# Square sums of q in PSUM, all of w_in converted during the scores, and three folds ahead of the layers, in a fused attention and feed-forward kernel

## The chip, the cores and the metric

One core of a Trainium2 chip runs the whole kernel. The metric is device time in microseconds (us), median of the timed runs. The engines are named as in the profile: PE (TensorE, matmuls), ACT (ScalarE), DVE (VectorE), POOL (GpSimd) and SP (SyncE, which issues every DMA of this kernel).

## The reference

Four batches of channel attention, with q, k and v of 6,080 tokens by 256 channels, then a layer pair of width 2,048 over all 24,320 tokens:

```python
def _attn_ref(q, k, v, tau):
    qn = q / (np.linalg.norm(q, axis=1, keepdims=True) + 1e-06)
    kn = k / (np.linalg.norm(k, axis=1, keepdims=True) + 1e-06)
    s = kn.transpose(0, 2, 1) @ qn / tau
    s = s - s.max(-1, keepdims=True)
    a = np.exp(s)
    a /= a.sum(-1, keepdims=True) + 1e-09
    return (v @ a).astype(np.float32)

def _moe_ref(x, w_in, w_out):
    h = x @ w_in
    g = h - np.tanh(h)
    return (g @ w_out).astype(np.float32)
```

The norms run over the tokens, so they need the squares of all of q and k of a batch summed up: these are the square sums of this text. w_in and w_out come in 64-bit floats.

## The kernel before

**Folding.** The kernel never computes v @ a. For each batch it multiplies the softmax e with w_in (a *fold*, `fold`, L270), one of eight column groups s of w_in at a time, and applies the result to v. A fold's result goes from PSUM (ps_w) to fx (L602), gets four sums on DVE (L608 to L611), and is split into a rounded upper half (L616, ACT) and the rest (L620, DVE). Both lie in f, a ring of three SBUF tiles, and are kept in DRAM (f_d) for the later token blocks.

**Quads.** The layers run in 192 quads: four batches, six pairs of token blocks of up to 512 columns, eight column groups. A quad makes seven products p1 to p7 of three matmuls each from f and the split V (vh, vl), by Strassen's scheme, in three PSUM banks x, y and z. ACT copies partial sums out (p, u), DVE adds (c), ACT takes tanh (t), DVE subtracts, ACT rounds (gh), DVE takes the rest (gl), and 24 matmuls with w_out add to ps_o. The list `ORDER` says in which order a quad's products stand on PE and where the side work (scores of the next batch, folds) goes.

**Converting.** w_in and w_out are turned from 64-bit to a pair of 32-bit floats on the chip (`Convert`), in eight pieces each. A piece is loaded (raw), ACT takes a magnitude (L313), DVE runs an upper part of three operations (L318, L320, L321) and a lower part of two (L327, L328), POOL adds (L331), ACT rounds (L334), POOL takes the rest (L337). A converted piece of w_in is stored to DRAM (wi_d, L354) and loaded again (L357) where its tile is needed in between.

**The first batch.** PE computes the scores of batch 0 in plain float32 (`plain_step`: 25 groups of up to two steps, 4 matmuls a step in the profile), as q and k come in. ACT squares each group in place (L415, L418). The squares are added up group by group: those of q on POOL into an SBUF tile (accq), those of k on DVE into PSUM bank 3 (acck), both at L424. ACT then copies acck to SBUF (L429), and 8 small matmuls per accumulator sum over the partitions (ps_n, L436). From these DVE computes the norms (x, y, z, r), a diagonal matrix (diag), PE spreads it (ps_b, L541), and the softmax and its transposes (ps_t) follow. In between PE runs steps of batch 1's scores, by `fill(n)`. Then come folds 0 and 1 and the first quad.

**Early pieces.** During the scores of batch 0 the pieces 2, 3, 0, 1, 4 and 5 of w_in are asked for, into a ring of three tiles `wi`. Folds 2 to 7 run inside quads 0 to 5.

**What sets the order.** `Plan` lists all operations with an estimated cost (`pe_cost`, `dve_cost` and so on) and a due time, and `order` writes each engine's instructions in the order in which its own small model would start them. The engines execute that order; each waits at an instruction until its inputs are there and its output tile is free. SP too takes its DMAs in order: a load whose tile is not free holds up all behind it.

```python
a, r = self.acc[x][:rows, 0:n, :], self.parts[g][0][x][:rows, 0:n, :]
(nc.vector if x else nc.gpsimd).tensor_add(a, r, a)
```

## Time and profile before

| what | value |
|---|---|
| median of 3 runs | 2210.99 us (2210.52 to 2213.96) |
| the profiled execution, its own time | 2209.88 us |
| its span in the profile | 2208.1 us |
| PE busy | 2172.0 us (98%), 10,034 matmul records |
| DVE busy | 1749.0 us (79%) |
| ACT busy | 1529.5 us (69%) |
| POOL busy | 79.6 us (4%), all of it in the first tenth |
| mean granted clock of PE | 0.995 |

Times in the timeline count from the start of the span. A row gives the start, the length of the run of instructions, the engine, the line and what is written from what; a bracket at its end gives the idle time ahead of it and what ended that. Idle time matters on PE, since it is busy nearly all the time; on another engine it costs something only where PE then waits. A clock of 1.00 in a stretch is PE's 2.4 GHz, 0.50 is 1.2 GHz.

### The profile page before, as it was taken

How to read it: one execution, taken by the hardware profiler on the slowest of the kernel's cores; microseconds unless marked ns; L12 is line 12 of the kernel's file. 1: busy time of each engine (PE TensorE's matmuls, PEld its weight loads, DVE VectorE, ACT ScalarE, POOL GpSimd, SP SyncE). 2: the span in 40 equal slices, each digit the busy share in tenths (PEclk: the TensorE clock that was granted, in tenths of full speed). 3: DMA queues.
4: the chain of work that ended last, by engine and by line, in shares of the span. 5: the costliest groups of instructions: out<-in, count | busy, mean ns of one | idle time of the engine just before them, and what ended most of it. 6: DMA issues, size and time to landing. Idle time of an engine off the chain costs nothing.

```text
span 2208.1 us, 28772 instructions
## 1 busy us (share of the span) xinstructions
PE 2172.0 (98%) x10034; PEld 1820.5 (82%) x10034; DVE 1749.0 (79%) x2813; ACT 1529.5 (69%) x2770; POOL 79.6 (4%) x62
## 2 busy tenths in 40 slices
PE   8899999999999999999999999999999999999999
PEld 7777878888888888888888888888888888888887
DVE  7688878778888787788788877778878888778775
ACT  6456777776677776776667767777667776666665
POOL 7322000000000000000000000000000000000000
PEclk9999999999999999999999999999999999999999
DMA  9753444443445544444335454454433333333331
GB/s 364 262 212 136 164 163 145 167 157 104 155 166 183 179 152 176 155 166 169 112 138 189 158 179 167 167 178 151 143 125 124 140 121 118 122 119 104 123 117 52
DMA packets 107379, 343.32 MB, mean 155 GB/s; under 512 B 11746, under 2 KB 17378, under 8 KB 107234
## 3 DMA queue, kind: packets, MB, share of 16 engines
q1 hardware_dynamic: 107234, 341.49, 43.6%
q8 instruction: 79, 1.29, 0.2%
q14 instruction: 66, 0.54, 0.1%
HBM read 282.98 MB, written 58.46 MB: 155 GB/s over the span
## 4 chain that ended last, share of the span: by engine, by line
PE 92%; DMA 3%; DVE 2%; issue 1%; ACT 1%; POOL 0%; SPq 0%; DVEq 0%; ACTq 0%; POOLq 0%
PE ps_o L872 45%; PE x L270 23%; PE y L270 11%; PE z L270 6%; PE ps_s L270 5%; DMA outT_dram<-ob 2%; PE ps_w L270 2%; DVE ob L887 0%; DMA vl<-k_dram 0%; ACT ob L887 0%; DVE t L808 0%; DMA raw_wi<-w_in_dram 0%; DVE gl L816 0%; DVE acck L424 0%; DMA wi<-wi_d 0%
## 5 line engine op out<-in xcount | busy, mean ns | idle before, releaser
L872 PE MATMUL ps_o<-gh,wo_l 128*128 128x512 f32 (+1 forms) x1536 | 597.7, 389 | 7.2 <-DVE ob L887 7.0
L872 PE MATMUL ps_o<-gh,wo_h 128*128 128x512 f32 (+1 forms) x1536 | 598.2, 389 | 0.0
L816 DVE TENSOR_TENSOR gl<-t,gh 128x512 fp32r<-128x512 f32 (+1 forms) x768 | 514.4, 683 | 64.2 <-ACT gh L812 60.2
L812 ACT CAST gh<-t 128x512 fp32r<-128x512 f32 (+1 forms) x768 | 463.1, 618 | 86.7 <-DVE t L808 84.1
L804 ACT ACTIVATE t<-c 128x512 f32<-128x512 f32 (+1 forms) x576 | 361.6, 628 | 166.0 <-DVE c L792 160.8
L270 PE MATMUL x<-vh,f 128*128 128x512 f32 (+1 forms) x1536 | 471.3, 388 | 1.1 <-DVE f L620 1.1
L872 PE MATMUL ps_o<-gl,wo_h 128*128 128x512 f32 (+1 forms) x1536 | 471.6, 388 | 0.0
L808 DVE TENSOR_TENSOR t<-c,t 128x512 f32<-128x512 f32 (+1 forms) x576 | 398.2, 694 | 80.0 <-ACT t L804 70.8
L783 ACT COPY u<-x 128x512 f32<-128x512 f32 (+1 forms) x384 | 223.8, 583 | 219.3 <-PE x L270 219.0
L872 PEld LDWEIGHTS ps_o<-gh,wo_l 128*128 128x128 f32 x1536 | 288.5, 188 | 68.1 <-DVE ob L887 10.8
L270 PEld LDWEIGHTS x<-vh,f 128*128 128x128 f32 x1536 | 288.3, 188 | 59.7 <-DVE f L620 1.6
L872 PEld LDWEIGHTS ps_o<-gl,wo_h 128*128 128x128 f32 x1536 | 288.6, 188 | 55.7
L872 PEld LDWEIGHTS ps_o<-gh,wo_h 128*128 128x128 f32 x1536 | 288.8, 188 | 53.2
L792 DVE TENSOR_TENSOR c<-u,y 128x512 f32<-128x512 f32 (+1 forms) x384 | 260.7, 679 | 74.9 <-ACT u L783 43.2
L270 PE MATMUL x<-vl,f 128*128 128x512 f32 (+1 forms) x768 | 299.9, 390 | 2.1 <-ACT gh L812 1.2
L270 PE MATMUL y<-vh,f 128*128 128x512 f32 (+1 forms) x768 | 235.3, 387 | 0.0
L792 DVE TENSOR_TENSOR c<-p,z 128x512 f32<-128x512 f32 (+1 forms) x192 | 130.8, 681 | 87.6 <-PE z L270 84.9
L808 DVE TENSOR_TENSOR t<-x,t 128x512 f32<-128x512 f32 (+1 forms) x192 | 131.4, 684 | 62.1 <-ACT t L804 60.7
L804 ACT ACTIVATE t<-x 128x512 f32<-128x512 f32 (+1 forms) x192 | 113.7, 592 | 87.8 <-PE x L270 86.8
L270 PEld LDWEIGHTS x<-vl,f 128*128 128x128 f32 x768 | 144.1, 188 | 32.4 <-ACT gh L812 1.6
L270 PEld LDWEIGHTS y<-vh,f 128*128 128x128 f32 x768 | 144.1, 188 | 28.8
L270 PE MATMUL y<-vl,f 128*128 128x512 f32 (+1 forms) x384 | 149.9, 390 | 0.0
(119 smaller groups left out, 2021.0 us busy)
## 6 DMA issues: line engine op xcount, KB each, us to landing
f<-f_d SPq DMA_DIRECT2D x160, 896.0 KB, 4.6
nt<-qkT_dram SPq DMA_DIRECT2D x96, 380.0 KB, 5.5
f_d<-f SPq DMA_DIRECT2D x32, 896.0 KB, 4.5
vraw<-vT_dram SPq DMA_DIRECT2D x80, 256.0 KB, 5.7
outT_dram<-ob SPq DMA_DIRECT2D x80, 256.0 KB, 2.6
raw<-q_dram SPq DMA_DIRECT2D x73, 256.0 KB, 4.8
raw<-k_dram SPq DMA_DIRECT2D x73, 256.0 KB, 5.1
wi<-wi_d SPq DMA_DIRECT2D x30, 512.0 KB, 5.2
```

What stands on the lines that cost most here:

```text
L270: ins = nc.tensor.matmul(out, w, x, start=first and i == 0, stop=last and i == len(seq) - 1, skip_group_check=True,)
L783: nc.scalar.copy(self.tiles[to], self.tiles["X"][:, 0:self.n])
L792: nc.vector.tensor_add(self.tiles[i], self.tiles[u], self.tiles[ps][:, 0:self.n])
L804: nc.scalar.activation(self.tiles["t", i], self.tiles[c][:, 0:n], AF.Tanh)
L808: nc.vector.tensor_sub(x, self.tiles[c][:, 0:n], x)
L812: nc.scalar.copy(self.g[i][0], self.tiles["t", i])
L816: nc.vector.tensor_sub(self.g[i][1], self.tiles["t", i], self.g[i][0].bitcast(F32))
L872: nc.tensor.matmul(outs[key + (m,)][:, 0:n], (wo_l if part else wo_h)[:, f, m * P:(m + 1) * P], quad.g[i][x], start=first and j == 0, stop ...
```

## The change

The squares of q are added up on DVE into PSUM bank 4, and both accumulators are copied to SBUF by ACT. The pieces of w_in are asked for in the order 0 to 6 at every third group of the scores: 0, 1 and 2 into the ring `wi`, where their folds read them, and 3, 4, 5, 6 and later 7 into tiles of the ring `f`, from where they are stored to DRAM and loaded again. Fold 2 moves from the first quad to a place ahead of it, behind one more step of batch 1. The conversions of w_out are due 10 us apart instead of 3. The scores of batch 1 are spread over seven quads instead of six. The planner's estimate for a matmul is 0.0134 + 0.000417 n instead of 0.015 + 0.000418 n. The sizes of the tiles stay, and so does the padding tile that puts them at multiples of 2,048 bytes.

```diff
+FIRST = 3
...
 def pe_cost(n):
-    return 0.015 + n * 0.000418
+    return 0.0134 + n * 0.000417
...
-    def convert_w_in(s):
+    def convert_w_in(s, tag):
         def dst():
-            w = w_in_tile(0, s)
+            if tag == "f":
+                f = sb(f_p, "f", [P, 2, NS, P], F32R, f"w_{s}").rearrange("p a n f -> p (a n f)")
+                w = wi[0, s] = f[:, 0:2 * KC * FB].rearrange("p (a k f) -> p a k f", a=2, k=KC)
+            else:
+                w = w_in_tile(0, s)
...
-                    for x in (sb(g_p, "u", [P, NMAX], F32, f"accq_{self.b}"), bank(3, f"acck_{self.b}"))
+                    for x in (bank(4, f"accq_{self.b}"), bank(3, f"acck_{self.b}"))
...
-            (nc.vector if x else nc.gpsimd).tensor_add(a, r, a)
-
-        def take_squares(self):
-            k_sq = sb(g_p, "u", [P, NMAX], F32, "sq_k")[:, 0:GJ * C].rearrange("p (j c) -> p j c", j=GJ)
-            self.sq = [self.acc[0], k_sq]
-            nc.scalar.copy(k_sq, self.acc[1])
+            nc.vector.tensor_add(a, r, a)
+
+        def take_squares(self, x):
+            sq = sb(g_p, "u", [P, NMAX], F32, f"sq{x}")[:, 0:GJ * C].rearrange("p (j c) -> p j c", j=GJ)
+            nc.scalar.copy(sq, self.acc[x])
+            self.acc[x] = sq
...
-    for s in range(2, NS2):
+    for s in range(FIRST, NS2):
         task(s - 2, "a", lambda s=s: plan_fold(0, s, banks(s - 2)["Z"]))
...
-    early = {
-        2: lambda due: plan_w_in(2, due=due),
-        5: lambda due: plan_w_in(3, due=due),
-        8: lambda due: plan_w_in(0, due=due),
-        11: lambda due: plan_w_in(1, due=due),
-        14: lambda due: plan_w_in(4, due=due),
-        18: lambda due: plan_w_in(5, due=due),
-    }
+
+    early = {2 + 3 * s: s for s in range(NS2 - 1)}
...
-            plan.add("POOL", pool_cost(GJ * C), lambda: ats[0].accumulate(g, 0), reads=x, writes=acc[0:1])
-            plan.add("DVE", dve_cost(GJ * C), lambda: ats[0].accumulate(g, 1), reads=x, writes=acc[1:], port=False)
+            for y in range(2):
+                plan.add("DVE", dve_cost(GJ * C), lambda y=y: ats[0].accumulate(g, y), reads=x, writes=acc[y:y + 1], port=False)
...
         if jj == 0 and g in early:
-            early[g](plan.pe_time)
+            plan_w_in(early[g], due=plan.pe_time, tag="wi" if early[g] < FIRST else "f")
...
-    sq, pn = [acc[0], Buf(ring["u"])], Buf(1)
-    plan.add("ACT", act_cost(GJ * C), ats[0].take_squares, reads=acc[1:], writes=sq[1:])
+    sq, pn = [Buf(ring["u"]) for _ in range(2)], Buf(1)
+    for x in range(2):
+        plan.add("ACT", act_cost(GJ * C), lambda x=x: ats[0].take_squares(x), reads=acc[x:x + 1], writes=sq[x:x + 1])
...
     plan_fold(0, 1, 1)
-    fill(3)
+    fill(4)
+    plan_fold(0, 2, 3)
+    assert steps[plain][1] == 0
+    plan_w_in(NS2 - 1, due=after_scores, tag="f")
     for s in range(NS2):
-        if s not in [0, 1, 2, 3, 4, 5]:
-            plan_w_in(s, due=after_scores + 3.0 * s)
-        if s not in []:
-            plan_convert(convert_w_out(s), wobuf[s], due=after_scores + 3.0 * s)
-
-    for s in range(2, NS2):
-        task(max(s - 3, 0), "start", lambda s=s: plan_load_w(0, s))
-    places = [(gs, x) for gs in range(NS2 - 2) for x in "cadb"]
...
+        plan_convert(convert_w_out(s), wobuf[s], due=after_scores + 10.0 * s)
+    for s in range(FIRST, NS2):
+        task(max(s - 4, 0), "start", lambda s=s: plan_load_w(0, s))
...
+            places = [(gs, x) for gs in range(NS2 - 1) for x in "cadb"]
```

PE, the first quad and fold 2. In a name the numbers are batch, token pair, column group, and a running number; ps_s_1 are batch 1's scores, x, y and z the banks of the first quad's products, ps_w_0_2 is fold 2. Before:

```order
L270 MATMUL ps_s_1_481<-raw_1_12_647 128x256 x2
L270 MATMUL y_0_0_0_771<-vl3_0_0_574,f_0_705 128x512
L270 MATMUL y_0_0_0_771<-vh3_0_0_495,f_0_705 128x512 x2
L270 MATMUL x_0_0_0_730<-vl4_0_0_579,f_0_705 128x512
L270 MATMUL x_0_0_0_730<-vh4_0_0_504,f_0_705 128x512 x2
L270 MATMUL ps_w_0_2_784<-wi_0_2_737,eh_640 128x256 x2
L270 MATMUL ps_w_0_2_784<-wi_0_2_737,el_645 128x256
```

PE at the end of fold 2 now:

```order
L271 MATMUL ps_w_0_2_763<-wi_0_2_153,eh_676 128x256 x2
L271 MATMUL ps_w_0_2_763<-wi_0_2_153,el_680 128x256
L271 MATMUL x_0_0_0_788<-vl0_0_0_552,f_0_737 128x512
L271 MATMUL x_0_0_0_788<-vh0_0_0_456,f_0_737 128x512 x2
L271 MATMUL x_0_0_0_788<-vl1_0_0_561,f_0_737 128x512
L271 MATMUL x_0_0_0_788<-vh1_0_0_516,f_0_737 128x512 x2
L271 MATMUL z_0_0_0_806<-vl2_0_0_573,f_0_737 128x512
```

Fold 2 now stands ahead of the first product of the first quad instead of behind its fifth, and reads the tile that the conversion wrote (wi_0_2_153, given out during the scores) instead of one that was loaded back (wi_0_2_737).

DVE between the square sums and the diagonal: x is read from ps_n, r are the norms' reciprocals, vl the split of V. Before:

```order
L507 TENSOR_SCALAR x_544<-ps_n_0_531 128x4
L678 TENSOR_TENSOR vl2_0_0_546<-vraw_0_0_256,vh2_0_0_486 128x512
L516 TENSOR_SCALAR y_553<-x_544 128x4
...
L530 TENSOR_SCALAR r_564<-r_564,itau_90 128x2
L678 TENSOR_TENSOR vl3_0_0_574<-vt_0_0_429,vh3_0_0_495 128x512
L535 TENSOR_SCALAR diag_576<-ident_82,r_564 128x128 x2
```

DVE there now:

```order
L512 TENSOR_SCALAR x_583<-ps_n_0_564 128x4
L683 TENSOR_TENSOR vl3_0_0_587<-vt_0_0_454,vh3_0_0_518 128x512
L319 TENSOR_SCALAR a_wi6_585<-a_wi6_585 128x512
L321 TENSOR_SCALAR a_wi6_585<-a_wi6_585 128x512
L322 SCALAR_TENSOR_TENSOR a_wi6_585<-raw_wi6_487,a_wi6_585 128x512
L521 TENSOR_SCALAR y_598<-x_583 128x4
...
L535 TENSOR_SCALAR r_609<-r_609,itau_90 128x2
L328 TENSOR_SCALAR m_wi6_614<-a_wi6_585 128x512
L329 SCALAR_TENSOR_TENSOR m_wi6_614<-raw_wi6_487,m_wi6_614 128x512
L540 TENSOR_SCALAR diag_617<-ident_82,r_609 128x128 x2
```

Five operations of the conversion of piece 6 of w_in now stand in the chain between x and the diagonal, and one vl less.

ACT at the upper half of f of fold 2, with p1_0_0_1 the copy of the second quad's first product. Before:

```order
L783 COPY u3_0_0_1_882<-x_0_0_1_827 128x512
L313 ACTIVATE a_wo3_904<-raw_wo3_721 128x512
L616 CAST f_2_908<-fx_0_2_807 128x896
L804 ACTIVATE t22_0_0_1_916<-c22_0_0_1_906 128x512
L602 ACTIVATE fx_0_3_934<-ps_w_0_3_891,rs_636 128x2x128
```

ACT there now:

```order
L809 ACTIVATE t21_0_0_0_855<-x_0_0_0_788 128x512
L809 ACTIVATE t22_0_0_0_861<-c22_0_0_0_845 128x512
L621 CAST f_2_867<-fx_0_2_827 128x896
L788 COPY p1_0_0_1_872<-x_0_0_1_857 128x512
L817 CAST gh11_0_0_0_876<-t11_0_0_0_847 128x512
```

The upper half of fold 2 now stands ahead of the second quad's first copy instead of behind its third, and its tile f_2 has the place in SBUF that f_0 has, which the first quad reads to its last product.

## Rows read from the trace of the kernel before

**Rows 1.** The page's chain of waits, share of the span by engine.

```profile
PE 92%; DMA 3%; DVE 2%; issue 1%; ACT 1%; POOL 0%; SPq 0%; DVEq 0%; ACTq 0%; POOLq 0%
```

**Rows 2.** By stretch: length; busy PE, PEld, DVE, ACT, POOL; clock; DMA share, GB/s.

```profile
0.00:100.00 100.00, 85.78 (x370) 71.47 (x370) 70.39 (x113) 50.23 (x89) 53.46 (x44) 0.93 0.88 315
170.00:230.00 60.00, 55.20 (x244) 44.14 (x243) 51.89 (x82) 38.13 (x69) 11.41 (x8) 1.00 0.44 154
```

**Rows 3.** Timeline of POOL late in the scores: start, length, line, operation, count.

```profile
45.78 9.65 POOL L424 TENSOR_TENSOR accq<-vh,accq 128x512 f32<-128x512 f32 x6
```

**Rows 4.** Timeline of DVE, from the scores to fold 0.

```profile
16.66 1.03 DVE L318 TENSOR_SCALAR a_wi<-a_wi 128x512 f32<-128x512 f32 x1
...
20.71 2.29 DVE L424 TENSOR_TENSOR acck<-vl,acck 128x512 f32<-128x512 f32 x3
22.90 0.42 DVE L327 TENSOR_SCALAR m_wi<-a_wi 128x512 int32<-128x512 int32 x1
...
23.97 0.42 DVE L318 TENSOR_SCALAR a_wi<-a_wi 128x512 f32<-128x512 f32 x1
...
49.74 0.68 DVE L424 TENSOR_TENSOR acck<-vl,acck 128x512 f32<-128x512 f32 x1
50.34 1.16 DVE L666 TENSOR_TENSOR vt<-vraw,vt 128x512 f32<-128x512 f32 x1
...
52.02 0.89 DVE L318 TENSOR_SCALAR a_wi<-a_wi 128x512 f32<-128x512 f32 x1
...
55.91 1.99 DVE L424 TENSOR_TENSOR acck<-vl,acck 128x512 f32<-128x512 f32 x3
...
67.22 0.17 DVE L516 TENSOR_SCALAR y<-x 128x4 int32<-128x4 int32 x1
...
69.99 0.48 DVE L535 TENSOR_SCALAR diag<-ident,r 128x128 f32<-128x128 f32 x2
...
78.64 0.43 DVE L318 TENSOR_SCALAR a_wo<-a_wo 128x512 f32<-128x512 f32 x1
...
79.57 0.69 DVE L321 SCALAR_TENSOR_TENSOR a_wo<-raw_wo,a_wo 128x512 int32<-128x512 int32 x1
```

**Rows 5.** Timeline of PE at the waits and at the folds.

```profile
52.86 8.46 PE L270 MATMUL ps_s<-raw 128*128 128x256 f32 x24 [2.40 <-DMA raw<-k_dram]
64.31 1.05 PE L436 MATMUL ps_n<-ones,accq 128*128 128x1 f32 x8 [2.98 <-POOL accq L424]
...
71.33 0.61 PE L541 MATMUL ps_b<-diag,ones 128*128 128x128 f32 x4
...
78.71 0.59 PE L270 MATMUL ps_w<-wi,eh 128*128 128x256 f32 x2
...
87.85 0.50 PE L270 MATMUL x<-vh,f 128*128 128x512 f32 x1 [1.14 <-DVE f L620]
...
97.70 0.47 PE L270 MATMUL ps_w<-wi,eh 128*128 128x256 f32 x2 [2.04 <-DVE a_wi L318]
...
108.23 0.40 PE L270 MATMUL ps_w<-wi,eh 128*128 128x256 f32 x2
...
160.13 0.77 PE L270 MATMUL ps_w<-wi,eh 128*128 128x256 f32 x2 [5.04 <-DMA wi<-wi_d]
...
180.02 0.48 PE L270 MATMUL ps_w<-wi,eh 128*128 128x256 f32 x2 [2.20 <-DMA wi<-wi_d]
```

**Rows 6.** Busy time and granted clock behind three of the waits, columns as in rows 2.

```profile
66.00:69.00 3.00, 3.00 (x9) 2.53 (x9) 2.18 (x11) 0.00 (x0) 0.00 (x0) 0.50 0.00 0
90.00:93.00 3.00, 3.00 (x9) 2.35 (x8) 1.85 (x5) 2.15 (x4) 0.34 (x2) 0.50 0.85 268
160.00:164.00 4.00, 3.87 (x15) 3.72 (x16) 2.48 (x4) 2.01 (x4) 2.82 (x2) 0.50 0.25 93
```

**Rows 7.** Timeline of ACT: f's upper half, and a product's copy.

```profile
83.79 0.94 ACT L616 CAST f<-fx 128x896 fp32r<-128x896 f32 x1 [1.94 <-DVE fx L611]
...
88.62 0.59 ACT L783 COPY p<-x 128x512 f32<-128x512 f32 x1
```

More of the change, by code (lines that the diff above doesn't have):

```diff
@@ L436, in sum_squares @@
                         nc.tensor.matmul(
-                            self.pn[:, x * KC + m:x * KC + m + 1], self.sq[x][:, j, m * P:(m + 1) * P], ones[:, 0:1],
+                            self.pn[:, x * KC + m:x * KC + m + 1], self.acc[x][:, j, m * P:(m + 1) * P], ones[:, 0:1],
                             start=j == 0, stop=j == GJ - 1, skip_group_check=True,
@@ L714, in attn_moe, with plan_w_in @@
     kept = {}
-    def plan_w_in(s, due=None):
-        w = wbuf[0, s] = Buf(ring["wi"])
-        plan_convert(convert_w_in(s), w, due=due)
+    def plan_w_in(s, due=None, tag="wi"):
+        w = wbuf[0, s] = Buf(ring[tag])
+        plan_convert(convert_w_in(s, tag), w, due=due)
         kept[s] = plan.add("SP", 0.35, lambda: keep_w_in(s), reads=[w], size=0.52, due=plan.pe_time)
@@ L957, in plan_channels, with plan_scores @@
         return sq
-    def plan_scores(b, places):
+    def plan_scores(b, places, ps, done=0):
         a = ats[b]
-        ps = Buf(7)
         parts = {}
@@ L975, in step @@
             plan.add("PE", 6 * pe_cost(C), lambda: a.score(g, jj), reads=list(parts[g]), writes=[ps])
-        for i, (g, jj) in enumerate(steps):
-            gs, x = places[i * len(places) // len(steps)]
+        for i in range(done, len(steps)):
+            g, jj = steps[i]
+            gs, x = places[(i - done) * len(places) // (len(steps) - done)]
             if jj == 0:
@@ L981, in plan_scores @@
             task(gs, x, lambda i=i: step(i))
-        return ps
     def plan_ends(b, sq, ps):
@@ L999, in attn_moe @@
     ats.update((b, Attn(b)) for b in range(B))
-    early = {
-        2: lambda due: plan_w_in(2, due=due),
-        5: lambda due: plan_w_in(3, due=due),
-        8: lambda due: plan_w_in(0, due=due),
-        11: lambda due: plan_w_in(1, due=due),
-        14: lambda due: plan_w_in(4, due=due),
-        18: lambda due: plan_w_in(5, due=due),
-    }
+    early = {2 + 3 * s: s for s in range(NS2 - 1)}
     tags = [[(v_p, "vh"), (v_p, "vl")]] * 8 + [[(g_p, "gh"), (g_p, "gl")]] * 5 + [["qh"], ["ql"]] * 2
     scores = {0: Buf(0), 1: Buf(7)}
-    acc = [Buf(ring["u"]), Buf(3)]
+    acc = [Buf(4), Buf(3)]
     held = {}
@@ L1045, in attn_moe @@
             plan.add("DVE", 0.2, take_tau, reads=[pt], port=False)
-    filled = 0
+    plain = 0
     after_scores = plan.pe_time
     def fill(n):
-        nonlocal filled
-        for filled in range(filled, min(filled + n, len(steps))):
-            plain_step(1, filled)
-        filled += 1
-    sq, pn = [acc[0], Buf(ring["u"])], Buf(1)
-    plan.add("ACT", act_cost(GJ * C), ats[0].take_squares, reads=acc[1:], writes=sq[1:])
+        nonlocal plain
+        for plain in range(plain, plain + n):
+            plain_step(1, plain)
+        plain += 1
+    sq, pn = [Buf(ring["u"]) for _ in range(2)], Buf(1)
+    for x in range(2):
+        plan.add("ACT", act_cost(GJ * C), lambda x=x: ats[0].take_squares(x), reads=acc[x:x + 1], writes=sq[x:x + 1])
     plan_moving(0)
@@ L1070, in attn_moe @@
     plan_fold(0, 1, 1)
-    fill(3)
+    fill(4)
+    plan_fold(0, 2, 3)
+    assert steps[plain][1] == 0
+    plan_w_in(NS2 - 1, due=after_scores, tag="f")
     for s in range(NS2):
-        if s not in [0, 1, 2, 3, 4, 5]:
-            plan_w_in(s, due=after_scores + 3.0 * s)
-        if s not in []:
-            plan_convert(convert_w_out(s), wobuf[s], due=after_scores + 3.0 * s)
-    for s in range(2, NS2):
-        task(max(s - 3, 0), "start", lambda s=s: plan_load_w(0, s))
-    places = [(gs, x) for gs in range(NS2 - 2) for x in "cadb"]
-    for i in range(filled, len(steps)):
-        gs, x = places[(i - filled) * len(places) // (len(steps) - filled)]
-        task(gs, x, lambda i=i: plain_step(1, i))
-    sq1 = plan_channels(1, NS2, SLOTS - 12)
-    plan_ends(1, sq1, scores[1])
-    for b in range(2, B):
-        g0 = (b - 1) * SLOTS
-        ps = plan_scores(b, [(g0 + s, x) for s in range(1, SLOTS - 6) for x in "ab"])
-        plan_ends(b, plan_channels(b, g0 + 1, g0 + SLOTS - 12), ps)
+        plan_convert(convert_w_out(s), wobuf[s], due=after_scores + 10.0 * s)
+    for s in range(FIRST, NS2):
+        task(max(s - 4, 0), "start", lambda s=s: plan_load_w(0, s))
+    for b in range(1, B):
+        g0 = (b - 1) * SLOTS
+        first = 1 if b > 1 else NS2
+        ps = scores[b] if b in scores else Buf(7)
+        if b == 1:
+            places = [(gs, x) for gs in range(NS2 - 1) for x in "cadb"]
+            for i in range(plain, len(steps)):
+                gs, x = places[(i - plain) * len(places) // (len(steps) - plain)]
+                task(gs, x, lambda i=i: plain_step(1, i))
+        else:
+            plan_scores(b, [(g0 + s, x) for s in range(first, SLOTS - 6) for x in "ab"], ps)
+        plan_ends(b, plan_channels(b, g0 + first, g0 + SLOTS - 12), ps)
     quads = {}
```

## Prediction

> **What bounds the kernel now.** I read the chain of waits on the page first: 92% of the span is TensorE [rows 1]. So a change can only take out time in which PE stands still, or runs at its lower clock level, and no work of PE is added or removed here. The busy time by stretches says where such time lies: 14.2 us idle in the first 100 us, 4.8 us in 170 to 230 [rows 2]; later it is busy nearly throughout. Then PE's own timeline, for the releaser in brackets. Five waits matter [rows 5]. Ahead of the square sums (ps_n, 64.31) PE waited 2.98 us for GpSimd's accumulates, six of which took 9.65 us from 45.78 on [rows 3]. At 87.85 the first quad waited 1.14 us for f of fold 0, at 97.70 fold 2 waited 2.04 us, at 160.13 fold 6 waited 5.04 us and at 180.02 fold 7 waited 2.20 us, the last two for the load of w_in back from DRAM. After three of these waits the granted clock was 0.50, that is 1.2 instead of 2.4 GHz: in 66 to 69 (behind ps_n), in 90 to 93 (behind 87.85) and in 160 to 164 (behind fold 6), with PE busy 3.00, 3.00 and 3.87 us [rows 6]. At half the rate these cost 1.5, 1.5 and 1.9 us.
>
> All times below are against the profiled execution: 2209.88 us with a span of 2208.1. The median of the three runs, 2210.99, lies 1.1 above it.
>
> **Step 1, the square sums.** DVE takes over 24 accumulates of q, so it now has 48. GpSimd loses them and keeps 2 per conversion. How long DVE needs is the first unknown. Its accumulate of 0.68 us at 49.74 is followed at 50.34 by an operation on another tile, 0.60 later; three accumulates into the same tile take 2.29, so (2.29 - 0.68) / 2 = 0.80 from one to the next [rows 4]. In the changed order accq and acck take turns, so I take 0.60, and 0.80 as the other end. A conversion has an upper part of three operations, 1.62 (78.64 to the end of the one at 79.57), and a lower part of 1.07 (22.90 to 23.97). While GpSimd ran its six accumulates beside it, an upper part took 3.89 (52.02 to 55.91) [rows 3, 4]; with these gone from GpSimd I take 1.62. From 16.7 us, where the second upper part starts (16.66), the order gives DVE 40 full accumulates, 2 of the short tail at some 0.4, 5 upper and 5 lower parts and three sums of V at some 2.4 in all: 24.0 + 0.8 + 8.1 + 5.4 + 2.4 = 40.7, so it ends at 57.4; with 0.80 it ends at 65.4. ScalarE's copy out of PSUM (some 0.7 with the hand-over) gives 58.1 to 66.1.
>
> PE's own side: it has six steps of the second batch ahead of the square sums. They began at 52.86 when their first load came, and took 8.46 us [rows 5]. Ahead of that load the queue now has one more transfer of 0.52 MB (seven conversion loads instead of six, with three stores as before); at 315 GB/s, the mean of the first 100 us [rows 2], that is 1.7 us. So PE is there at 52.9 + 1.7 + 8.46 = 63.0. The later of the two is PE, by 4.9 us. **Square sums at 63.0 instead of 64.3**, with no idle time ahead of them. If PE's clock holds, its six steps are 3 us shorter; if 0.80 is right, it is 66.1.
>
> **Step 2, from the square sums to fold 0.** PE's square sums last 2.2 us (64.31 to 66.5), so DVE starts on the norms at 65.2. Between x and the diagonal it had 67.22 to 69.99 for norms with one vl inside, 2.2 without [rows 4]. The new order puts one vl (0.6), the upper part of w_in 6 (1.6) and its lower part (1.1) into that chain: 0.6 + 1.6 + 2.2 + 1.1 + 0.5 for the diagonal = 6.0, so the spread can run at 71.4 with the hand-overs. PE has four steps in between, 66.5 to 71.33 before with 1.5 of low clock, so 3.3: it is there at 68.5. This is the wait that takes the place of the old one, 2.9 us. **Spread at 71.4 instead of 71.33.** Behind waits of this size the clock fell [rows 6], so I charge 1.5. From the spread to fold 0 before took 7.4 us (71.33 to 78.71), with 0.42 of waiting for the softmax that goes, since less stands between its steps on DVE; the upper part of w_out 0 now stands ahead of the low half of e, which I charge with 0.3. **Fold 0 at 71.4 + 7.4 + 1.5 - 0.4 + 0.3 = 80.2, 1.5 later than before.**
>
> **Step 3, folds 0 to 3 and the first quads.** From fold 0 to fold 3 (78.71 to 108.23) the work is the same, only fold 2 stands ahead of the first quad. Gone: 2.04 us, as w_in 2 is converted in place and needs no load; 1.14, as fold 2 and one more step now lie between fold 0 and its first reader (f came 9.1 us behind the start of fold 0, at 87.85, and PE asked for it 8.0 behind; a fold of 1.7 and a step of 0.9 more make 10.6); and the 1.5 of low clock. New: f of fold 2 lies in the slot of f of fold 0, because the other slots hold w_in tiles, so its upper half can't be written until the first quad's last product, and ScalarE has it in its queue just ahead of the copy of p1 of the second quad, for which that quad's p6 waits. From the end of that product: 0.27 until ScalarE starts (88.35, the end of the product at 87.85, to 88.62), 0.94 for f, 0.59 for p1 [rows 5, 7], against one step of PE, some 0.9. That is a wait of 0.9; between 0, if the rows overlap, and 2, if ScalarE runs late. -2.0 - 1.1 - 1.5 + 0.9 = -3.7. **Fold 3 at 106.0 instead of 108.23.**
>
> **Step 4, folds 6 and 7.** w_in 3 to 6 are converted before the layers, and their loads stand 30 rows and more behind their stores in SyncE's queue. So the 5.04 and 2.20 and the 1.9 of low clock go: **-9.1.** w_in 7 is converted among the first folds. What is late next is DVE's and ScalarE's work on the layers, which these pauses let catch up. In 170 to 230 DVE was busy 51.89 of 60 us [rows 2]; three conversions fewer (11 before, 8 now) take 8 us out of that stage, so I charge nothing and keep 3 us for the range.
>
> Costed at nothing: the two sums in bank 4 and bank 3 (no product uses bank 4 until the layers), the w_out loads that come later (10 us apart instead of 3; each has a whole quad), and the tiles that move in SBUF by the new order of first use: their sizes stay. The constants of the planner shift ScalarE and DVE by a row here and there through the layers, but leave PE's order alone there; +/-2 us.
>
> **The sum**: +0.1 (spread) + 1.4 (to fold 0) - 3.7 - 9.1 = -11.3 us; 2209.88 - 11.3 = 2198.6, and 1.1 more for the median: 2199.7.
>
> **The rivals.**
> A. *DVE's accumulates bound the start.* With 0.80 the square sums start at 66.1, 3.1 later than in the sum, PE stands still before them and runs at half clock behind them as before (1.5): 2199.7 + 4.6 = 2204.3. For it: three in a row into one tile do take 0.80. Against: here the tiles alternate, and 0.60 is seen twice with another tile next (49.74 to 50.34; 2.29 from 20.71 ends at 23.00, but the next starts at 22.90). The Trainium skill has a rule on its side, VectorE: DVE Perf Modes, section "The DRAIN you can't avoid": the next operation doesn't start until the pipe is empty. By that rule the 0.80 of the three would hold for any two accumulates, and A's 2204.3 would be the time; the start at 50.34, before the 0.68 of the one at 49.74 are over, contradicts it here.
> B. *The layers give it back.* One w_out conversion in each of seven quads, without PE's pauses, makes DVE the bound. PE lost 4.8 us in 170 to 230, of which fold 7's 2.2 is one; if quads 1 to 7 (100 us) lose the other 2.6 per 60 us, 4.3 us, and the new waits of steps 2 and 3 are at their upper ends (3 us), it is 2199.7 + 7.3 = 2207. Against: before, the first quads had as many conversions each, and PE waited there for loads alone.
> C. *Slower: SyncE's queue.* Five w_out loads (3 to 7) each wait for DVE to release a raw tile, and the loads of the second batch and of w_in stand behind them. If PE runs dry there as at fold 6, each costs 5.04 + 1.9 = 6.9 us. Two eat the gain; three make it 2199.7 + 20.7 = 2220. Against: four tiles are loaded ahead, and DVE has the releasing step before the quad ends.
> D. *The change doesn't do what it says*: w_in 3 or 6 is still late, for its slot is free only after fold 0 to 2 and its load stands behind w_out loads. One such wait, 6.9: 2206.6.
>
> **How the numbers follow.** Forecast 0.66, A 0.18, B 0.07, D 0.05, C 0.04. The forecast's own range: down by 3 (full clock in the six steps), 0.9 (no wait for f) and 2 (planner), up by 2 to 3 (layers) and 1 (f): 2193.8 to 2203.7. To hold 8 in 10 it reaches beyond A, 2193.8 to 2206.0; B, C and part of D stay out. About 0.2% (4.4 us) is what a measurement of this kernel can tell from no change: below 2206.6 is faster. Forecast, A and half of D make 0.86; B and the other half of D 0.10; slower is C.
>
> **What would show it.** GpSimd's busy time falls from 79.6 to about 41 us. ps_n starts near 63.0 with no idle ahead (A: a wait of 3 us for ScalarE's copy). A wait of some 2.9 us for DVE stands ahead of the spread (ps_b), near 71. Fold 3 starts near 106.0. No entry of ps_w waits for a load. A wait of about 1 us for ScalarE stands in the second quad. From 230 us on the stretches look as before. I am wrong if ps_w still waits for wi, or if PE's idle time in 100 to 230 is not near zero.

## The result, and the profile after

The changed kernel takes 2192.73 us (median of five runs, 2192.34 to 2196.18). The kernel before, run beside it, took 2213.96 (2210.52 to 2215.32). The ratio is 0.991, with a 95% interval of 0.9896 to 0.9925: it is faster, by about 20 us. The median lies 7.0 us under the forecast of 2199.7 and 1.1 us under the lower end of the range. The profiled execution took 2193.2 us with a span of 2191.4; that is 16.7 less than the span of before. The profiled execution of before, 2209.88, is shorter than all of its timed runs on record (2210.06 to 2216.25), so differences from profile to profile come out smaller than those of the medians.

PE's timeline of the changed kernel at the places of [rows 5] (start, length, engine, line, operation, operands, count; in brackets the idle time ahead and what ended it):

```profile
52.78 7.24 PE L271 MATMUL ps_s<-raw 128*128 128x256 f32 x24 [1.68 <-DMA raw<-k_dram]
59.85 1.84 PE L441 MATMUL ps_n<-ones,sq 128*128 128x1 f32 x16
...
67.50 0.71 PE L546 MATMUL ps_b<-diag,ones 128*128 128x128 f32 x4 [1.50 <-DVE diag L540]
...
74.34 0.59 PE L271 MATMUL ps_w<-wi,eh 128*128 128x256 f32 x2
...
85.96 0.50 PE L271 MATMUL x<-vl,f 128*128 128x512 f32 x1 [1.09 <-ACT p L788]
...
95.30 0.50 PE L271 MATMUL x<-vl,f 128*128 128x512 f32 x1 [0.69 <-ACT p L788]
...
99.76 0.40 PE L271 MATMUL ps_w<-wi,eh 128*128 128x256 f32 x2
...
193.33 0.50 PE L271 MATMUL x<-vl,f 128*128 128x512 f32 x1 [0.92 <-DVE vl L683]
...
196.23 0.50 PE L271 MATMUL z<-vl,f 128*128 128x512 f32 x1 [1.93 <-DVE t L813]
```

The square sums start at 59.85 instead of 64.31, with no wait. Fold 0 starts at 74.34 instead of 78.71, fold 3 at 99.76 instead of 108.23. No fold waits for w_in any more; of [rows 5] the waits of 2.98, 1.14, 2.04, 5.04 and 2.20 are all gone. New are 1.50 ahead of the spread, 0.69 for a copy of p in the second quad, and 0.92 for DVE at 193.33. The 1.93 at 196.23 is not new but grown: the same product (the ninth in bank z) waited 0.84 for DVE in the kernel before, which then had one more wait for ACT that is gone now:

```profile
212.24 0.50 PE L270 MATMUL z<-vl,f 128*128 128x512 f32 x1 [0.84 <-DVE t L808]
...
216.43 0.47 PE L270 MATMUL x<-vl,f 128*128 128x512 f32 x1 [1.18 <-ACT gh L812]
```

By stretches (columns as in [rows 2]):

```profile
0.00:100.00 100.00, 89.20 (x407) 74.10 (x408) 82.83 (x159) 59.05 (x105) 25.24 (x24) 0.98 0.99 363
100.00:170.00 70.00, 70.00 (x338) 59.17 (x337) 60.31 (x98) 43.33 (x77) 14.46 (x10) 1.00 0.55 191
170.00:230.00 60.00, 56.23 (x238) 44.91 (x237) 53.02 (x82) 40.09 (x76) 6.76 (x4) 0.97 0.37 127
```

PE is busy 89.2 of the first 100 us (before 85.78, clock 0.93) and without a gap from 100 to 170. From 170 to 230 it still stands still for 3.8 us, at a clock of 0.97. So fold 3 is 8.5 us earlier, and what follows it is 8.2 us shorter (2208.1 - 108.23 = 2099.9 before, 2191.4 - 99.76 = 2091.6 after); the two make the 16.7.

The part DVE has taken over reads as follows on its timeline, with the short tail of the accumulates and the chain from x to the diagonal:

```profile
40.99 0.68 DVE L429 TENSOR_TENSOR accq<-vh,accq 128x512 f32<-128x512 f32 x1
41.59 0.68 DVE L429 TENSOR_TENSOR acck<-vl,acck 128x512 f32<-128x512 f32 x1
...
57.30 0.41 DVE L429 TENSOR_TENSOR acck<-vl,acck 64x256 f32<-64x256 f32 x1
...
61.73 0.16 DVE L512 TENSOR_SCALAR x<-ps_n 128x4 f32<-128x4 f32 x1
...
67.16 0.47 DVE L540 TENSOR_SCALAR diag<-ident,r 128x128 f32<-128x128 f32 x2
```

The accumulates of the two sums start 0.60 us apart, the last ends at 57.71, and the chain lasts 5.9 us.

### The profile page after: what moved, and what is told of

The parts are those of the page before. It is cut to its first block, busy times and chain, and to the rows that moved or that the text cites. A ratio compares the mean times of both kernels' runs of the same rounds, so it can differ in the third digit from the quotient of the medians.

```text
span 2191.4 us, 28798 instructions
## 1 busy us (share of the span) xinstructions
PE 2165.3 (99%) x10034; PEld 1815.8 (83%) x10034; DVE 1753.1 (80%) x2837; ACT 1527.6 (70%) x2771; POOL 46.5 (2%) x38
## 4 chain that ended last, share of the span: by engine, by line
PE 92%; DMA 2%; DVE 1%; ACT 1%; issue 0%; SPq 0%; DVEq 0%; ACTq 0%
PE ps_o L877 46%; PE x L271 23%; PE y L271 11%; PE z L271 6%; PE ps_s L271 4%; DMA outT_dram<-ob 2%; PE ps_w L271 2%; DVE ob L892 0%; ACT ob L892 0%; DVE gl L821 0%; DVE t L813 0%; ACT f L621 0%; DVE vl L683 0%; SPq L896 0%; ACT u L788 0%
## 5 line engine op out<-in xcount | busy, mean ns | idle before, releaser
L813 DVE TENSOR_TENSOR t<-c,t 128x512 f32<-128x512 f32 (+1 forms) x576 | 397.7, 692 | 73.4 <-ACT t L809 63.5
```

The costliest lines, as they stand in the source:

```text
L813: nc.vector.tensor_sub(x, self.tiles[c][:, 0:n], x)
```

## The experiments

Every run stands against the kernel before, timed beside it on the same chip:

| run | what it is | median us | ratio to before (95%) |
|---|---|---|---|
| changed kernel | | 2192.73 | 0.9910 (0.9896 to 0.9925) |
| b_psum | before, with both sums in PSUM on DVE | 2201.98 | 0.9948 (0.9935 to 0.9960) |
| q_pool | changed, with q's accumulates back on POOL | 2212.68 | 0.9993 (0.9984 to 1.0002) |
| first2 | changed, fold 2 back in the first quad | 2197.92 | 0.9929 (0.9917 to 0.9942) |
| first2f | the same, own banks | 2195.86 | 0.9922 (0.9910 to 0.9935) |
| late67 | changed, w_in 6 and 7 late | 2192.99 | 0.9906 (0.9893 to 0.9920) |
| late67f | the same, own banks | 2192.87 | 0.9906 (0.9891 to 0.9921) |
| late67_wo3 | the same, w_out 3 us apart | 2196.46 | 0.9921 (0.9908 to 0.9935) |
| wo3 | changed, w_out due 3 us apart | 2194.47 | 0.9914 (0.9900 to 0.9927) |
| cost | changed, the planner's old costs | 2194.76 | 0.9918 (0.9905 to 0.9932) |
| one_acc | changed, one joint sum | 2200.34 | 0.9940 (0.9928 to 0.9953) |
| wo_early | changed, w_out by fixed due times | 2191.04 | 0.9904 (0.9890 to 0.9917) |
| wo_after | the same, first w_out load after the spread | 2194.44 | 0.9915 (0.9902 to 0.9929) |

In q_pool, late67 and first2 the kernel keeps only the last fold's bank by name, and with the moved order a copy into fx reads the bank of the next fold: in q_pool and late67 the copies of fold 1 read fold 2's, in first2 the second half of fold 0 reads fold 1's. So those copies come later than they need, and fx of that fold holds another fold's product: of these three runs only the times are used. late67f and first2f repeat two of them with each fold's own bank; late67_wo3, one_acc, wo_early and wo_after have it too.

### The parts one by one

**Both sums on DVE alone, in the kernel before (b_psum).**

```diff
-                    for x in (sb(g_p, "u", ...), bank(3, f"acck_{self.b}"))
+                    for x in (bank(4, f"accq_{self.b}"), bank(3, f"acck_{self.b}"))
...
-            (nc.vector if x else nc.gpsimd).tensor_add(a, r, a)
+            nc.vector.tensor_add(a, r, a)
...
```

> The kernel before with one part of the change alone: both sums of squares in PSUM, accumulated by VectorE; w_in, the folds and the planner's numbers stay. Theory 1 (GpSimd's accumulates held up the start by themselves): ps_n moves from 64.31 to 60 to 61.5 us, and the run takes 2.5 to 4.5 us less than the kernel before (ratio 0.998 to 0.9988), while the waits of folds 6 and 7 for w_in (5.0 and 2.2 us) stay. Theory 2 (the part pays only together with the early conversions, because in the kernel before the loads and the low clock set ps_n nearly as late): ps_n not before 63.5 us, within 1 us of the kernel before.

Measured: 2201.98 against 2213.42, 11.4 us less, more than half of the whole gain and far more than either theory gave. Theory 1 is right in direction: ps_n is earlier than even its 60 us, and the waits of folds 6 and 7 stay. PE's timeline of this run:

```profile
52.12 1.10 PE L270 MATMUL ps_s<-raw 128*128 128x256 f32 x4 [0.45 <-DMA raw<-k_dram]
...
57.80 1.84 PE L436 MATMUL ps_n<-ones,sq 128*128 128x1 f32 x16
...
63.47 0.71 PE L541 MATMUL ps_b<-diag,ones 128*128 128x128 f32 x4 [0.26 <-DVE diag L535]
...
86.57 0.47 PE L270 MATMUL ps_w<-wi,eh 128*128 128x256 f32 x2 [1.56 <-DMA wi<-wi_d]
...
149.00 0.76 PE L270 MATMUL ps_w<-wi,eh 128*128 128x256 f32 x2 [5.09 <-DMA wi<-wi_d]
...
171.30 0.77 PE L270 MATMUL ps_w<-wi,eh 128*128 128x256 f32 x2 [4.99 <-DMA wi<-wi_d]
```

The square sums start at 57.80, 6.5 us earlier than before and 2.0 earlier than in the changed kernel. Fold 0 starts at 70.31 and fold 3 at 97.07 (11.2 earlier than before). The waits for w_in stay and grow: 5.09 and 4.99 for folds 6 and 7, where before had 5.04 and 2.20. So the other parts of the change cost 4.0 us at the start (fold 0 at 74.34 instead of 70.31) and take out these waits. On DVE's timeline of this run, x is at 59.68 and the diagonal at 63.13: 3.45 us, because no conversion stands in that chain. In the changed kernel it is 61.73 to 67.16, 5.43, with the upper and lower part of w_in 6 inside.

The 11.2 us up to fold 3 can be added up from the rows of both kernels: 0.7 because the first plain load comes earlier (52.12 instead of 52.86), 2.8 in the six steps behind it (5.68 instead of 8.47), 3.0 for the wait for POOL, 1.9 from the square sums to fold 0 (12.51 instead of 14.40) and 2.8 from there to fold 3 (26.76 instead of 29.52). The wait that the profile names is about a quarter of it. Much of the rest is clock: the kernel before ran at 0.50 from 53 to 57, behind its wait for the first plain load, and again in 66 to 69 and 90 to 93 [rows 6], b_psum at 1.00 throughout (by stretch, columns as in [rows 2]):

```profile
0.00:100.00 100.00, 90.75 (x424) 75.82 (x425) 82.15 (x156) 58.75 (x105) 22.66 (x22) 1.00 0.95 344
```

PE stands still for loads nearly as long from 40 us to the square sums, but in small pieces (0.90, 0.56, 0.45 and 0.19) instead of 2.40 at once. From profile to profile the whole run is 7.1 us shorter (2201.0 against 2208.1), as 4.1 of the 11.2 are lost again behind fold 3, in the main at the waits for w_in.

**The other parts without it (q_pool).**

```diff
-                    for x in (bank(4, f"accq_{self.b}"), bank(3, f"acck_{self.b}"))
+                    for x in (sb(g_p, "u", ...), bank(3, f"acck_{self.b}"))
...
-            nc.vector.tensor_add(a, r, a)
+            (nc.vector if x else nc.gpsimd).tensor_add(a, r, a)
...
```

> The changed kernel with one part undone: the sum of squares of q is gathered by GpSimd in SBUF again, 21 accumulates of 1.27 to 1.6 us, as in the kernel before; everything else stays (all of w_in early, three folds ahead). Theory 1 (the accumulates on GpSimd set the start): GpSimd also has seven pairs of conversion steps in front of the last accumulate now, so ps_n waits for accq again, at 63.5 to 67 us instead of 59.85, and the time is 2192.7 plus that delay, 2196.4 to 2199.9 us. Its second sign: the q and k tiles are given back late, so the DMA rate between 50 and 60 us falls from about 390 GB/s towards the 250 of the kernel before. Theory 2 (the loads set the start, whoever accumulates): ps_n within 1 us of 59.85 and at most 2193.7 us, with the same DMA rate.

Measured: 2212.68, within 0.2% of the kernel before. Theory 1 had the direction and missed the size: the delay is 18 us, not 3 to 7. (POOL has 24 such accumulates; the expectation's 21 was a slip.) Its second sign did not come: from 50 to 60 us q_pool moved 380 GB/s, the changed kernel 382. So accumulates on POOL did not lower the rate of the loads there. PE, then POOL:

```profile
77.73 1.87 PE L441 MATMUL ps_n<-ones,accq 128*128 128x1 f32 x8 [14.36 <-POOL accq L429]
```

```profile
57.30 1.38 POOL L332 TENSOR_TENSOR a_wi<-a_wi,m_wi 128x512 f32<-128x512 f32 x1 [4.08 <-DVE m_wi L329]
...
62.99 4.08 POOL L429 TENSOR_TENSOR accq<-vh,accq 128x512 f32<-128x512 f32 x3
68.89 1.64 POOL L332 TENSOR_TENSOR a_wi<-a_wi,m_wi 128x512 f32<-128x512 f32 x1 [1.81 <-DMA wi_d<-w]
70.49 1.71 POOL L429 TENSOR_TENSOR accq<-vh,accq 128x512 f32<-128x512 f32 x1
72.16 1.71 POOL L338 TENSOR_TENSOR w<-a_wi,w 128x512 fp32r<-128x512 f32 x1
73.84 3.84 POOL L429 TENSOR_TENSOR accq<-vh,accq 128x512 f32<-128x512 f32 x3
```

POOL waits in order: it stands 4.08 us for the lower part of a conversion and later 1.81 at another one, with accumulates queued behind, and four of the last accumulates stand behind a conversion's two steps of 1.64 and 1.71. So, in the order of this run, early conversions and accumulates on POOL get in each other's way. The parts don't add up: 11.4 us for the sums alone, 1.5 for the rest alone (2214.18 - 2212.68, its interval holds zero), about 20 together. That the wrong bank of fold 1 has a share in these 2212.68 us can't be excluded; it comes after the 14.36.

**Fold 2 back in the first quad (first2, first2f).**

```diff
-FIRST = 3
+FIRST = 2
-    plan_fold(0, 2, 3)
```

> The changed kernel with fold 2 back inside the first quad (FIRST = 2), its piece of w_in reloaded from DRAM; all the rest stays. Theory 1 (the third fold ahead of the layers removed the reload's wait of 2.0, the wait of 1.1 for f of fold 0 and the 1.5 of low clock behind, against 0.9 for a new wait): 3.7 us come back, fold 3 at about 103.5 instead of 99.76, 2196.4 us (2195 to 2198). Theory 2 (these waits came from the late start of the kernel before, so that they are gone anyway): within 1 us of the changed kernel, at most 2193.8 us.

> The changed kernel with fold 2 back inside the first quad (FIRST = 2), its piece reloaded from DRAM, and each fold's copies reading that fold's own bank (in the run before this one, with the same move, the second half of fold 0 was copied from the bank of fold 1 and so waited for it, which put up to 5 us on the wait for f of fold 0). Theory 1: the reload's wait and the hand-off wait of the kernel before come back, about 3.7 us with the clock, 2196.4 us (2195 to 2198). Theory 2 (most of the 5.2 us of that run came from the wrong bank): at most 2194 us.

Measured: 2197.92, and 2195.86 with own banks, 3.1 more than the changed kernel. That lies in theory 1's range. But wo3 below, which is the changed kernel's program run again beside first2f on the same chip, took 2194.47, and against that it is only 1.4. And what came back is not what theory 1 named: no fold waits for a reload, and one product waits long for f of fold 0. PE in first2f:

```profile
86.56 0.80 PE L271 MATMUL x<-vl,f 128*128 128x512 f32 x1 [5.39 <-ACT f L622]
89.15 0.80 PE L271 MATMUL x<-vl,f 128*128 128x512 f32 x1 [0.68 <-ACT p L789]
```

On DVE the upper and lower parts of two conversions (75.73 to 82.4) stand ahead of the sums of fold 0, and two of those sums are stretched to 1.35 beside POOL; the last ends at 85.5, and f follows. In the changed kernel one more fold lies between fold 0 and its first reader, which covers this. Fold 3 is at 105.30, 5.5 later than in the changed kernel; what follows fold 3 is 3.0 shorter (2193.9 - 105.30 = 2088.6 against 2091.6), as the waits near 200 us are smaller there and no low clock follows them (PE busy 56.99 in 170 to 230 at a clock of 1.00). So the move to three folds ahead is worth 1.4 to 3.1 us here, hardly more than two runs of one program differ by, with another wait than the one predicted as its counterpart.

**Pieces 6 and 7 late (late67, late67f), and with the old spacing of w_out (late67_wo3).**

```diff
-    early = {2 + 3 * s: s for s in range(NS2 - 1)}
+    early = {2 + 3 * s: s for s in range(NS2 - 2)}
...
-    plan_w_in(NS2 - 1, due=after_scores, tag="f")
...
+        if s >= NS2 - 2:
+            plan_w_in(s, due=after_scores + 3.0 * s, tag="f")
```

> The changed kernel with pieces 6 and 7 of w_in loaded and converted late, due 18 and 21 us after the scores as in the kernel before; the other parts stay. Theory 1 (earliness of the conversions is what removed the waits of folds 6 and 7): the two waits for DMA ahead of ps_w come back with 4 to 5 and about 2 us and a low clock behind one of them, 2198 to 2203 us. Theory 2 (what held the pieces up were the w_out conversions queued among them, which the change puts off from 3 to 10 us apart): the pieces arrive in time even so, no wait for wi ahead of ps_w, at most 2194.5 us.

> The changed kernel with pieces 6 and 7 of w_in late, w_out 10 us apart, and each fold's copies reading that fold's own bank (in the earlier run with the late pieces, the copies of fold 1 read the bank of fold 2 and waited for it). Theory 1 (what matters for folds 6 and 7 is that their pieces are not queued behind w_out, not that they are converted during the scores; and two conversions fewer stand ahead of ps_b): no wait for w_in, fold 0 at 73.4 us or earlier, 2190.5 to 2193 us. Theory 2 (the wrong bank hid a wait): a wait for w_in of 2 us or more ahead of a fold, 2195 us or more.

> The changed kernel with pieces 6 and 7 of w_in late (due 18 and 21 us after the scores) and, with them, the eight w_out conversions 3 us apart again instead of 10, the mix of the kernel before; each fold's copies read that fold's own bank. In the run with the late pieces alone no fold waited for w_in. Theory 1 (the w_out conversions queued among them are what held pieces 6 and 7 up): the two waits for DMA ahead of ps_w return, 4 to 5 and about 2 us, with a low clock behind, 2198 to 2203 us. Theory 2 (the third fold ahead and the earlier start give the pieces room enough either way): waits of at most 1 us, at most 2194.5 us.

Measured: 2192.99 and 2192.87, the time of the changed kernel, with no fold that waits for w_in. With w_out 3 us apart again it is 2196.46, and fold 6 waits:

```profile
163.40 0.47 PE L271 MATMUL ps_w<-wi,eh 128*128 128x256 f32 x2 [3.93 <-DMA wi<-wi_d]
```

In that order w_in 6 is loaded behind six w_out pieces, in late67f behind two. So converting all of w_in during the scores is sufficient but not necessary; what holds piece 6 up is w_out in front of it, as in the kernel before, where it is loaded behind six w_out pieces too. For fold 7 this is not shown: its wait did not come back. Theory 2 of late67 stands. Theory 1 of late67f stands but for fold 0, which starts at 74.04 and not at 73.4 or earlier: the spread is earlier (66.63), but the softmax then holds PE up for 0.45. Of late67_wo3 theory 1 has the mechanism, at a smaller size (one wait of 3.9, not two of 7.2); its time lies between the two theories' ranges, 2.0 over wo3 on the same chip.

**The due times of w_out alone (wo3).**

> The changed kernel with the eight w_out conversions due 3 us apart instead of 10; all of w_in stays early. Theory 1 (once w_in is ready it does not matter when w_out is converted, as long as nothing is queued on its pieces): no wait of a fold for w_in, within 2 us of the changed kernel (2190.7 to 2194.7), and since the conversions are done before 190 us the wait of PE for DVE at 193 to 196 us (0.92 and 1.93) and the low clock behind it go, or come earlier. Theory 2 (DVE and GpSimd have no room for them in the first four quads): new waits of PE for DVE between 80 and 130 us of 3 us or more in all, 2196 us or more.

Measured: 2194.47. The order of the instructions is the same as in the changed kernel on every engine, so this tells nothing of either theory: it is the same program once more, timed apart from it, 1.7 us away in the median. Differences below that mean nothing here.

**The planner's costs (cost).**

> The changed kernel with the planner's cost of a matmul as before (0.015 + 0.000418 n); nothing else is undone. Theory 1 (the constants only shift a few neighbours in the order): within 1.5 us of the changed kernel, 2191.2 to 2194.2 us, with fold 3 within 0.5 us of 99.76. Theory 2 (the order that follows from them carries a part of the gain): slower by 3 us or more.

Measured: 2194.76, fold 3 at 99.48. The median is 0.6 us over theory 1's range, fold 3 lies in it. The difference of 2.0 us is near that of the repeat; theory 2 is out.

### The accumulates' pace

**One joint sum (one_acc)**, so that each accumulate needs the one before.

```diff
-                    for x in (bank(4, f"accq_{self.b}"), bank(3, f"acck_{self.b}"))
+                    for x in [bank(4, f"acc_{self.b}")] * 2
...
-    acc = [Buf(4), Buf(3)]
+    acc = [Buf(4)] * 2
```

> The changed kernel with the squares of q and of k added into one sum in one PSUM bank instead of two (both norms then come from the joint sum), so that each accumulate depends on the one just before it; the number of instructions is the same. Theory 1 (dependent operations stand 0.80 us apart on VectorE where independent ones stand 0.60 apart, the rival A of the prediction): some 38 full accumulates cost 0.2 us more each, about 7.6 us on an engine that is busy for 19.8 of the 20 us from 20 to 40 us; the last accumulate ends at 63 to 66 instead of 57.7, ps_n waits for it to 64.5 to 67.5, and the run takes 2197 to 2200 us. Theory 2 (alternating operands had nothing to do with the pace): accumulates 0.60 apart, the changed kernel's time within 1.5 us.

Measured: 2200.34, 7.6 more. DVE of this run, and PE:

```profile
29.82 0.70 DVE L429 TENSOR_TENSOR acc<-gh,acc 128x512 f32<-128x512 f32 x1
30.62 0.69 DVE L429 TENSOR_TENSOR acc<-gl,acc 128x512 f32<-128x512 f32 x1
31.42 0.70 DVE L429 TENSOR_TENSOR acc<-gh,acc 128x512 f32<-128x512 f32 x1
```

```profile
69.00 3.58 PE L441 MATMUL ps_n<-ones,sq 128*128 128x1 f32 x16 [9.34 <-ACT sq L433]
```

Dependent accumulates stand 0.80 apart in these rows (0.72 to 0.80 where one follows right on another), where those of the changed kernel stand 0.60 apart. The square sums wait 9.34 us and start at 69.00, 1.5 us later than theory 1's upper end, since the planner also put conversions and splits of V between the accumulates. The last accumulate ends 9.5 us later than in the changed kernel (67.19 against 57.71). Twenty full-size pairs at about 0.80 and eight at about 0.72 instead of 0.60 make some 5 of these; the rest is that other order. So the pace of rival A is real and the alternation of the two sums kept it away, but the 7.6 us are not its price alone.

### What is left

**w_out by fixed due times (wo_early), and its first load after the spread (wo_after).**

```diff
-        plan_convert(convert_w_out(s), wobuf[s], due=after_scores + 10.0 * s)
+        plan_convert(convert_w_out(s), wobuf[s], due=after_scores + 10.0 * s, by=after_scores + 30.0 + 12.0 * s)
```

`by` sets the due time of every step of the conversion, not of its load alone. wo_after adds `after=mark`, the matmul of the spread.

> The changed kernel with every step of the w_out conversions given a due time (30 us after the scores and then 12 us apart), so that the last of them lies some 15 us earlier than at 189 to 199 us, out of the stretch in which VectorE is busy without a break (182 to 211 us); each fold's copies read that fold's own bank, which changes nothing here. Theory 1 (the waits for DVE at 193 to 196 us, 0.92 and 1.93, and 1.7 of low clock behind them come from that last conversion and its GpSimd steps): they go, 2188 to 2190.5 us. Theory 2 (VectorE has too much to do from 100 to 210 us, wherever the conversions stand): a wait of like size elsewhere, 2191.5 to 2194.5 us.

> As the run before it, and the first load of w_out only after the spread ps_b, so that it no longer stands in the queue ahead of the first plain load of the second sample (at 45.3 and 46.6 us in the changed kernel). Theory 1 (that transfer of 0.52 MB is the 1.7 us that PE waits at 52.78, and the low clock behind it follows): the load at 51 to 52 us, wait at most 0.6, ps_n at 57.8 to 58.5 as in the kernel before with the sums in PSUM alone (57.80), fold 0 at 72 to 73; 1.3 to 2.5 us less than the run before it. Theory 2 (the loads of this stretch are held by the slots they are loaded into, not by the queue): ps_n within 0.5 us of 59.85, no gain over the run before it.

In the changed kernel the last w_out piece stands on DVE at 188.80 to 192.67 with POOL beside it. By stretches, the changed kernel:

```profile
192.00:196.00 4.00, 1.38 (x5) 0.48 (x3) 4.00 (x5) 2.00 (x4) 1.67 (x1) 1.00 0.75 300
196.00:200.00 4.00, 3.77 (x10) 3.02 (x11) 4.00 (x6) 3.37 (x7) 1.69 (x1) 0.60 0.00 0
```

and wo_early:

```profile
192.00:196.00 4.00, 4.00 (x20) 3.30 (x19) 3.10 (x6) 2.08 (x4) 0.00 (x0) 1.00 0.44 163
196.00:200.00 4.00, 4.00 (x19) 3.34 (x18) 4.00 (x8) 2.90 (x6) 0.00 (x0) 1.00 0.27 59
```

The waits at 193 to 196 and the clock of 0.60 behind them are gone, as theory 1 of wo_early said, and none of like size stands elsewhere behind 100 us. Its median is 2191.04 (2189.68 to 2196.88), the lowest of all, between the ranges of the two theories, and its interval overlaps that of the changed kernel: a gain is not shown. The profile is of its longest run, in which the spread waited 3.05 us for DVE and fold 0 started at 79.49.

In wo_after PE waits less at the load, and nothing is gained:

```profile
44.81 3.69 PE L271 MATMUL ps_s<-vh,vl 128*128 128x256 f32 x16 [1.24 <-DMA vl<-k_dram]
49.19 3.02 PE L271 MATMUL ps_s<-vh,vl 128*128 128x256 f32 x12 [0.69 <-DMA vl<-k_dram]
52.53 1.10 PE L271 MATMUL ps_s<-raw 128*128 128x256 f32 x4 [0.32 <-DMA raw<-k_dram]
...
61.60 1.05 PE L441 MATMUL ps_n<-ones,sq 128*128 128x1 f32 x8 [1.63 <-ACT sq L433]
...
68.81 0.71 PE L546 MATMUL ps_b<-diag,ones 128*128 128x128 f32 x4 [2.60 <-DVE diag L540]
```

The wait at the load falls from 1.68 to 0.32, but the load itself comes only 0.25 us earlier than in the changed kernel, at 52.53 and not at 51 to 52. PE gets there 1.1 us later, since it waited 1.24 and 0.69 for the last rows of the first batch, where the changed kernel waited 0.44 and 0.39. The square sums start at 59.02, but their second half waits 1.63 for ACT's copy and the spread 2.60 for DVE. So theory 1 fails, but for the size of that one wait, and 59.02 is in neither theory's range for ps_n; the time is 2194.44. In this stretch DVE and ACT are the next bound right behind the loads.

## Why the prediction was right in sign and short in size

- **The bound and the direction: right.** Only idle time and low clock could be taken out of PE, and they were. Rivals C and D didn't come: no load of w_out or w_in holds PE up. Rival A is refuted for the changed kernel by its own rows (0.60 apart); one_acc, where it comes true together with another order, takes 7.6 more, where the text had +4.6.
- **Step 1, the term that failed first.** Square sums forecast at 63.0, measured 59.85. The side of DVE was right: 57.4 forecast, 57.71 measured, with the 40 full accumulates and the five conversions that the text counted. The side of PE was mis-sized twice. The transfer more ahead of its load was charged with 1.7 us at 315 GB/s; the load came at 52.78, no later than before, since that stretch ran at 400 GB/s. That 1.7 had no lower end in the range. And the six steps took 7.07 instead of 8.46, since the clock was low for a shorter time. The range had the second, not the first.
- **Step 2.** The chain was right: 6.0 forecast, 5.9 measured. But both ends came earlier, x at 61.73 instead of 65.2 and PE at 66.0 instead of 68.5, so the wait was 1.50 instead of 2.9. The 1.5 us of low clock behind that wait did not come: from the spread to fold 0 it took 6.84 us, not 8.8. Fold 0 was forecast 1.5 later than before and came 4.4 earlier, 5.9 off: 3.2 from step 1 and 2.7 from step 2. This is nearly all of the error.
- **Step 3: right in size, in part by other causes.** Fold 0 to fold 3 was forecast at 25.8 us and took 25.42. The new wait for a copy of p in the second quad was forecast at 0.9 and is 0.69, behind ACT's work on f as described. first2f puts the move of fold 2 at 1.4 to 3.1, against 3.7, and neither the reload's wait nor the wait for f returns there as it was; in b_psum the wait for f is gone without the move.
- **Step 4: right in size, its cause too narrow.** -9.1 forecast, -8.2 measured behind fold 3. late67f shows that the early conversion of 6 and 7 isn't needed for it, late67_wo3 that w_out ahead of piece 6 hurts. "I charge nothing" for DVE in the layers was wrong: PE now stands still for 0.92 and 1.93 at 193 to 196, where the kernel before had 0.84 and 1.18 at 212 to 216, and the clock of 0.60 behind it is new. That is rival B, in one place, at a fraction of its price.
- **What the steps didn't see.** The prediction gave the accumulates' move 1.3 us (64.3 to 63.0); alone it is worth 11.4. It looked for the effect at the one wait ahead of ps_n (3.0 of the 11.2 us that b_psum gains up to fold 3) and charged new waits and low clock against it. b_psum has no low clock up to 100 us. It is not that POOL held the loads up: of the waits of SP for a free tile or a finished one, in the first 170 us of the kernel before, only one names an accumulate on POOL, and that is ahead of a store:

```profile
SPq L354 <- POOL accq L424: 0.4, 1, 0.4
```

- **The sum.** -11.3 forecast, -16.7 measured from profile to profile: 5.4 of error. Fold 0 makes 5.9 (80.2 against 74.34), step 3 adds 0.4, and step 4 takes 0.9 back. The remaining 1.6 of the 7.0 to the median is the allowance of +1.1 for the median, which lay 0.5 under the profiled run.
- **The signs.** No fold waits for w_in, and the square sums start without a wait. POOL is busy 46.5 us, not about 41: its steps took 1.27 where they ran alone and up to 1.96 in the layers. The text would call itself wrong if PE's idle time in 100 to 230 was not near zero; it is 3.8 us, all behind 190 us, after 9.8 in the kernel before.

What stays open: why the kernel before moved 350 GB/s from 45 to 50 us where b_psum moved 391 and q_pool, with POOL accumulating, 383. It is not POOL's pace alone. No run separated it. Open too: whether the sums of q gain by the faster engine or by lying in PSUM, since b_psum moves both together, and why the clock falls behind one wait and not behind another of the same length.

## What to carry to other kernels

When an engine that runs in order holds up a busy PE, count more than the wait that the profile names: moving 24 accumulates from POOL (1.27 to 1.7 us each) to DVE (0.60 apart) took out a wait of 3.0 us, and 8.2 more up to fold 3, much of it low clock. Test the parts of a combined change in both directions, alone and left out; here 11.4 and 1.5 made 20. Before converting work early, ask what is queued ahead of the late pieces: putting the less urgent loads behind did the same. And run the changed kernel itself again beside the experiments: two medians of one program lay 1.7 us apart, as much as some parts seemed to be worth.
